# A planned attention and expert kernel: transfers booked in order, loads held back, v in rows of 128 tokens

## The chip, the core and the metric

The kernel runs on one NeuronCore of one Trainium2 chip. The core has a matrix engine (TensorE, PE in the profile, with its weight loads shown apart as PEld), a vector engine (VectorE, DVE), a scalar engine (ScalarE, ACT), a general engine (GpSimd, POOL) and SyncE (SP), which issues nearly all transfers here. The metric is device microseconds of one execution; lower is better. The kernel before took 566.9 us, the median of 3 runs from 564.42 to 567.85.

## The reference

Three layers follow each other; all inputs but the third layer's weights are float32.

1. Attention by landmarks, for 4 batches of 8 heads with 576 tokens and head size 64. 32 landmarks of q and of k are means over 18 tokens. With sm the softmax over scaled products: A = sm(q, k_lm), Bm = sm(q_lm, k_lm), C = sm(q_lm, k). Z is the inverse of Bm by six rounds of Z = 2Z - Z Bm Z. The result is A Z C v.
2. A layer of 8 experts. A router picks one expert for each of the 2304 tokens (rows of 512); each expert takes at most `capacity` tokens, in order. Its result is `relu(x w1) w2`, 512 to 1024 to 512, times the router's probability.
3. A gated unit on all rows: `(sigmoid(x w_gate) * (x w_val)) w_out`, 512 to 1536 to 512.

## The kernel before, in words

Each (batch, expert) pair that holds tokens is a unit of work: all 576 tokens of the batch are taken through that expert and the gated unit, and the rows that belong to the expert are scattered into `out`. In these inputs three such units show in the trace: "lead" (batch 0), "1" (batch 1) and "2". The lists of units are computed on the chip, and a loop at the end runs over what is left.

**Attention.** q and k of a batch come in four tiles of two transfers each (`load_qk`, `slot` tiles for batches 0 and 1, `qk` tiles for 2 and 3), v in one tile `vs` with one buffer (`load_v`). `sums` adds up the landmarks `ld`, `inverse` makes Bm (`pb`) and runs the six rounds (`pz`, tile `rz`), `context_parts` makes the scores of C (`pc`), `context_part` their exponentials (`ec`), `context_turn` transposes these with TensorE (`pct`) and copies them to SBUF (`ct`), and `context` multiplies them by v (`pv`). In the kernel before a tile row of `ct` and `vs` is one of 96 groups of 6 tokens, so that there are 2 x 3 transposes of 96 columns for each of two groups of heads, and 6 products for each head. `scores` and `weights` make A (`pa`, `ea`, `at`): maximum, subtraction, exponential, sum, normalisation and transposes. `back` joins Z and C v to `fold`, multiplies by the router's weights (`pw`) and gets each token's logits; `parts` splits A into two rounded parts that are the rows x of the expert layer (in the tiles `xa` and `xb` for batches 0 and 1), and `row_store` writes them and `fold` to memory, where a later unit reads them again.

**Lead experts.** `number` (`pl`) finds the expert of the first token of batch 0 and of batch 1. SyncE reads that number and loads the expert's 16 weight tiles of 256 KB (`expert_loads`, tile `w_raw`, four buffers). The first eight are multiplied by `fold` (`expert_fold`: products `mm<-w_raw,fold_now`), the others split into two rounded parts (`expert_split`, tile `ws`). `expert_products` then runs the hidden layer (`mm<-xa,ws`) and the w2 layer (`mm<-slot,ws`); `gated` scales its result by the gate (`yt`) and writes it over x in `xa`. So TensorE can work on the lead experts while the attention of the later batches is still under way. The third layer's weights are loaded, narrowed to float32 and used only after the attention (`narrow`, `unit_split`, `unit_products`, `unit_out`).

**The planner.** The order on each engine is written out by hand-made code, the class `Streams`. Each piece of work is a generator that yields the engine that it wants next and what it needs: names of events, or of buffers. `go` starts at every step the piece with the smallest sum of its possible start and `SLACK` (0.003 us) times its urgency, so 100 points of urgency are worth 0.3 us; a smaller number goes first. `settle` advances the engines' clocks by the costs in `COSTS`. A transfer is booked by `took("sp", ...)` and an event some fixed time later. An operation of GpSimd also costs VectorE 0.3 of its time (`SHARED`). `slow` guesses from the columns of recent products whether TensorE's clock would fall; then pieces marked `pe+` (dense products) go first, and `fill_up` puts products without use (`idle`) in front of a piece that would start late. The planner sets only the order: on the chip every instruction still waits for the data that it needs, and SyncE's queue runs in the order given.

Other names that matter: `SUBS` says which engine subtracts the maximum in `weights`, for each batch; `SUMS` which landmark sums run on GpSimd; `URGENCY` holds the urgencies.

Of the kernel before, what the change touches and what calls it, by code (L numbers as in the profile page):

```python
# [38 lines left out]
    lead_split=20,  # L39
    fold=0,  # L40
# [8 lines left out]
SUBS = ("pool", "pool", "dve", "dve")  # L49
NORMS = ("pool", "pool", "pool", "pool")  # L50
SLACK = 0.003
# [53 lines left out]
class Streams:  # L105
# [14 lines left out]
    MARGIN = 1.08  # L120
    SOON = 0.0
    SPAN = 3.4
    SHORTEST = 96

    def __init__(self, nc, slots):
# [6 lines left out]
        self.live = []  # L132
        self.busy = {}
# [19 lines left out]
    def took(self, engine, time):  # L153
        self.log.append(("run", engine, time, 0))

# [134 lines left out]
def tile_attention_moe_glu(  # L290
# [15 lines left out]
    B, P, H, J, DH = v.shape  # L306
    S = P * J
    N, D = out.shape
# [14 lines left out]
    REST = T % 128  # L323
    ENDS = [0, 1, *range(4, TC), 2, 3]
# [49 lines left out]
    nc.vector.tensor_reduce(eye, ident.rearrange("p (h m) -> p m h", m=LM), AX.X, ALU.add)  # L374
    shift = once.tile([128, 256], F32R, name="shift")
# [48 lines left out]
    def use(run):  # L424
        on.pe, on.dve, on.act, on.pool = run.pe, run.dve, run.act, run.pool
        on.later, on.took, on.release, on.done = run.later, run.took, run.release, run.done
# [59 lines left out]
    def gated(b, y, d, half, pt):  # L486
# [3 lines left out]
        yield "dve", "sg", f"gate_{b}"  # L490
# [32 lines left out]
    def narrow_all():  # L523
        for f in range(KG):
            cols = [w[f].bitcast(U32).rearrange("p k (f w) -> p k f w", w=2) for w in (w_gate, w_val)]
            rows = w_out[f].bitcast(U32).rearrange("p (k d w) -> p k d w", w=2, k=KD)
            for nm, res, src in zip("gvo", (wgs, wvs, wos), (*cols, rows)):
# [5 lines left out]
                on.took("sp", 2.1)  # L533
                on.done(f"raw_{nm}{f}", 2.5)
                run.spawn(narrow(res[f], raw, kind, f"{nm}{f}"), URGENCY["narrow"])

    def urgency(stage, b):
        if b == B - 1 and stage in ("inverse", "context", "back", "ranks"):
            return 0
        return URGENCY[stage] + (STEP * b - AHEAD * (b == 0) if b in range(B) else 0)  # L540
# [9 lines left out]
    def expert_loads(b, number, at, split_urgency, first=0, until=KF + 2 * KD, after=(), needs=()):  # L550
# [7 lines left out]
        for i in range(first, until):  # L558
# [8 lines left out]
            run.took("sp", 0.6)  # L567
            run.done(f"w_raw_{b}{i}", 2.2)
# [216 lines left out]
    def zero_rows():  # L785

        rows = out.rearrange("(p r) d -> p (r d)", p=128)
        for c in range(18):
# [6 lines left out]
            on.took("sp", 1.5)  # L795
# [7 lines left out]
    def block_x(b, number, x, *needs):  # L803
# [6 lines left out]
        on.took("sp", 2.5)  # L810
        for event in (f"fold_{b}", f"x_{b}0", f"x_{b}1", f"gate_{b}"):
            on.done(event, 6.0)
# [3 lines left out]
    with actx:  # L816
# [36 lines left out]
        def load_qk(b):  # L853
            for w, src in enumerate((q, k)):
                for g in range(G):
                    if b < 2:
                        t = slot(4 * b + 2 * w + g, F32)
                    else:
                        yield "sp", "qk"
                        t = wk.tile([128, 2, S], F32, tag="qk", name=f"qk{b}{w}{g}", bufs=6)  # L860
                    for kk in range(2):
                        yield ("sp",)
                        nc.sync.dma_start(t[:, kk], src[b, g, :, kk])
                        run.took("sp", 0.6)
                        run.done(f"raw{b}{w}{g}{kk}", 2.0)
# [9 lines left out]
        def load_v(b):  # L875
            yield "sp", f"raw{b}{1}{G - 1}1", f"context{b - 1}"
            vs = wk.tile([P, H, J, DH], F32, tag="vs", name=f"vs{b}", bufs=1)
            for h in range(0, H, 2):
                nc.sync.dma_start(vs[:, h : h + 2], v[b, :, h : h + 2])
            run.took("sp", 4.5)  # L880
            if b == 0:
                nc.sync.dma_start(wrt, w_router)
                nc.sync.dma_start(cap_i, capacity.bitcast(I32).partition_broadcast(128))
            st[b]["vs"] = vs
            run.done(f"v{b}", 2.0)
# [27 lines left out]
        def inverse(b):  # L913
# [52 lines left out]
            run.release("bank")  # L966
            yield ("dve",)
            dve.tensor_tensor(rz[:, :, 1], bb[:, 0], rn.unsqueeze(2).broadcast_to([128, G, LM]), ALU.mult)

            for it in range(NS_ITERS):  # L970
                last = it == NS_ITERS - 1
                yield "pe", "bank", *([f"square{b}{it - 1}"] if it else [])
                pr = pst([128, G, 2, LM], f"pz{b}{it}")
                for h in range(H):
                    o, g = (h % 4) * 32, h // 4
                    of = slice(1, 2) if last else slice(0, 2)
                    pe.matmul(pr[o : o + 32, g, of], rz[o : o + 32, g, 0], rz[o : o + 32, g, of], start=True, stop=True)
                new = wk.tile([128, G, LM] if last else [128, G, 2, LM], F32, tag="zl" if last else "rz", name=f"rz{b}{it}")
                if not last:
                    run.later([("act", lambda new=new, pr=pr: act.copy(new[:, :, 0], pr[:, :, 0]))], free(done=[f"square{b}{it}"]))  # L980
                yield ("dve",)
                dve.tensor_tensor(
                    new if last else new[:, :, 1], rz[:, :, 1], pr[:, :, 1], ALU.add if it else ALU.subtract
                )
# [66 lines left out]
        def context(b):  # L1051
            yield None, f"context{b - 1}"
            ct = st[b]["ct"] = wk.tile([P, G, 2, 3, 128], F32, tag="ct", name=f"ct{b}", bufs=1)
# [5 lines left out]
            for g in range(G):  # L1059
                for u in range(2):  # L1060
                    yield "pe", f"ct{b}{g}{u}", *(["bank"] if g == u == 0 else [])
                    if g == u == 0:
                        pv = pst([128, G, DH], f"pv{b}")
                    for jj in range(3):
                        for i in range(H // G):
                            o = place(H // G * g + i)[2]
# [43 lines left out]
        def context_part(b, g, pcs):  # L1110
# [8 lines left out]
            for u in range(2):  # L1119
                yield "act", "ec"  # L1120
                ec = wk.tile([128, HT], F32, tag="ec", name=f"ec{b}{g}{u}")
                act.activation(ec, pcs[u], AF.Exp, bias=nb, scale=SA, accum_out=sums[:, u : u + 1])
# [4 lines left out]
        def context_turn(b, g, u, ec):  # L1127
# [434 lines left out]
```

## Time and profile before

| | |
|---|---|
| median of 3 runs | 566.9 us (564.42 to 567.85) |
| profiled execution | 566.14 us |
| its span | 564.3 us, 12363 instructions |
| TensorE busy | 543.3 us, 96% (weight loads 489.7 us, 87%) |
| VectorE, ScalarE, GpSimd busy | 346.6 us (61%), 251.1 us (44%), 82.3 us (15%) |
| transfers | 61.86 MB, mean 110 GB/s |
| products without use (`idle`) | 18, 10.9 us, all before 27 us |

The profile is of one execution. Busy times are sums over instructions; matmuls are pipelined, so the span of a group of them divided by their count is the better price of one, and "mean ns" is how long one is in the pipe. The page's own chain of what ended last is short here, as it stops at the last scatter; the argument goes by stages instead.

### The profile page before, as it was taken

To read this page: it belongs to the slowest core of one execution; us is meant where nothing else is said; L and a number is where in the kernel's file an instruction comes from. 1 tells how busy PE (TensorE), PEld (TensorE's weight loads), DVE (VectorE), ACT (ScalarE), POOL (GpSimd) and SP (SyncE) were. 2 spreads that over 40 slices of the span, in tenths; PEclk is the share of its full clock that TensorE was granted. 3 is DMA by queue.
4 is the path that set the end of the run, shared out by engine and by line. 5 is a ranking of instruction groups with operands and counts; after the bars stand their busy time and mean duration, and the time that the engine had idled before them with its cause. 6 is when DMAs were issued, how large, how long until landed. Compare 5 with 4: busy or idle time off the path is not lost. (4 is left out here: it accounts for less than half of the span.)

```text
span 564.3 us, 12363 instructions
## 1 busy us (share of the span) xinstructions
PE 543.3 (96%) x4938; PEld 489.7 (87%) x4938; DVE 346.6 (61%) x824; ACT 251.1 (44%) x564; POOL 82.3 (15%) x100
## 2 busy tenths in 40 slices
PE   8889899999999999999999999999999999999994
PEld 3457768888998999999899999998999999999993
DVE  7877698877699988897453434343565534344431
ACT  1446434453577767674243333343443333333430
POOL 2662743242210000000120000001200000000012
PEclk9979899997999999999999999999999999999998
DMA  8998276685654544440520000002520000000002
GB/s 283 312 290 274 77 234 190 211 230 196 243 150 150 201 173 156 180 154 2 187 77 1 1 1 0 1 1 66 186 59 1 0 1 1 1 1 1 2 19 70
DMA packets 32479, 61.86 MB, mean 110 GB/s; under 512 B 3648, under 2 KB 13504, under 8 KB 32416
## 3 DMA queue, kind: packets, MB, share of 16 engines
q1 hardware_dynamic: 31312, 57.48, 32.2%
q0 software_dynamic: 1104, 3.54, 1.8%
q8 instruction: 40, 0.66, 0.5%
q14 instruction: 23, 0.19, 0.1%
HBM read 47.76 MB, written 13.25 MB: 108 GB/s over the span
## 5 line engine op out<-in xcount | busy, mean ns | idle before, releaser
L100 PE MATMUL mm<-xa,ws 128*128 128x288 f32 x1344 | 188.4, 297 | 0.9 <-ACT sg L100 0.8
L100 PEld LDWEIGHTS mm<-xa,ws 128*128 128x128 f32 x1344 | 183.3, 189 | 5.4 <-ACT sg L100 1.1
L100 PE MATMUL acc<-ws,slot 128*128 128x512 f32 x504 | 123.5, 392 | 0.0
L100 PEld LDWEIGHTS acc<-ws,slot 128*128 128x128 f32 x504 | 91.8, 188 | 17.5 <-issue 0.4
L100 PE MATMUL mm<-xb,ws 128*128 128x288 f32 x672 | 95.1, 300 | 0.0
L100 PEld LDWEIGHTS mm<-xb,ws 128*128 128x128 f32 x672 | 92.8, 192 | 1.7 <-PE mm L100 0.5
L100 PE MATMUL mm<-slot,ws 128*128 128x288 f32 x576 | 81.5, 298 | 0.0
L100 PEld LDWEIGHTS mm<-slot,ws 128*128 128x128 f32 x576 | 77.1, 188 | 2.8 <-issue 1.9
L100 ACT CAST slot<-sg 128x288 fp32r<-128x288 f32 x72 | 31.1, 432 | 66.7 <-DVE sg L100 66.4
L100 DVE TENSOR_TENSOR slot<-sg,slot 128x288 fp32r<-128x288 f32 (+2 forms) x108 | 35.4, 355 | 24.3 <-ACT slot L100 24.2
L100 DVE TENSOR_TENSOR sg<-mm,sg 128x288 f32<-128x288 f32 x72 | 32.7, 455 | 27.8 <-PE mm L100 20.4
L100 DVE TENSOR_TENSOR ws<-wo_res,ws 128x512 fp32r<-128x512 f32 x36 | 24.9, 692 | 35.4 <-ACT ws L100 35.4
L100 DVE TENSOR_TENSOR ws<-wg_res,ws 128x512 fp32r<-128x512 f32 x36 | 24.9, 691 | 27.1 <-ACT ws L100 27.1
L100 DVE TENSOR_TENSOR ws<-wv_res,ws 128x512 fp32r<-128x512 f32 x36 | 24.9, 691 | 24.5 <-ACT ws L100 24.3
L100 ACT CAST ws<-wo_res 128x512 fp32r<-128x512 f32 x36 | 22.4, 621 | 34.9 <-PE acc L100 28.4
L100 ACT CAST ws<-wg_res 128x512 fp32r<-128x512 f32 x36 | 22.3, 620 | 29.2 <-PE mm L100 28.4
L100 ACT CAST ws<-wv_res 128x512 fp32r<-128x512 f32 x36 | 22.3, 618 | 28.3 <-PE mm L100 27.4
L100 ACT ACTIVATE sg<-mm 128x288 f32<-128x288 f32 x72 | 29.0, 403 | 1.0 <-PE mm L100 0.9
L100 ACT ACTIVATE slot<-mm 128x288 fp32r<-128x288 f32 x48 | 19.6, 410 | 17.1 <-PE mm L100 16.5
L100 DVE TENSOR_TENSOR yt<-mm,gate_now 128x288 f32<-128x288 f32 x24 | 16.8, 701 | 16.7 <-PE mm L100 16.7
L770 POOL DMA_INDIRECT out<-o_tile,idx_two x5 | 4.8, 966 | 150.8 <-DVE o_tile L100 147.8
L100 POOL TENSOR_TENSOR ws<-w_raw,ws 128x512 fp32r<-128x512 f32 x16 | 20.9, 1304 | 37.3 <-ACT ws L100 37.3
(212 smaller groups left out, 541.4 us busy)
## 6 DMA issues: line engine op xcount, KB each, us to landing
w_raw<-in_moe_w SPq DMA_DIRECT2D x48, 256.0 KB, 4.6
raw_g<-in_moe_w_gate SPq DMA_DIRECT2D x12, 512.0 KB, 3.9
raw_v<-in_moe_w_val SPq DMA_DIRECT2D x12, 512.0 KB, 3.9
raw_o<-in_moe_w_out SPq DMA_DIRECT2D x12, 512.0 KB, 3.9
vs<-in_v SPq DMA_DIRECT2D x16, 288.0 KB, 7.6
out<-zeros SPq DMA_DIRECT2D x18, 256.0 KB, 3.7
slot<-in_q SPq DMA_DIRECT2D x8, 288.0 KB, 5.6
slot<-in_k SPq DMA_DIRECT2D x8, 288.0 KB, 5.7
```

What stands on the lines that cost most here:

```text
L100: return getattr(self.engine, op)(*args, **kwargs)
L770: scatter = nc.gpsimd.indirect_dma_start(out[:, :], bass.IndirectOffsetOnAxis(ap=idx[0:n, c : c + 1], axis=0), o[0:n], None, bounds_check= ...
```

## The change

1. The planner books transfers. `took("sp", ...)` and `done(event, delay)` of a transfer become `moved(bytes, *events)`: the transfer starts after the one before it, moves 0.36 MB per us and lands 0.64 us later; SyncE is booked until the eighth transfer before has landed (`LANES`).
2. Some transfers are held back (`HOLD`): q and k of batch 2 until the lead's weight tile 3 is in, those of batch 3 until tile 7, the row store of batch 0 until tile 15; that of batch 1 is not held.
3. Urgencies are other numbers, with an extra per batch (`EXTRA`), and `MARGIN`, by which `slow` asks for dense work, goes from 1.08 to 1.2.
4. `gated` waits for the row store of its batch before it writes over x ("rows0", "rows1").
5. The subtraction of the maximum goes to VectorE for batches 0 and 1 and to GpSimd for 2 and 3 (before: the other way round).
6. v is laid out on the host in order of tokens and loaded as rows of 512 numbers, 128 tokens to a tile row block, with three transfers a batch (512, 512 and 128 KB) for four of 288 KB. The context weights are turned in five transposes (four of 128 columns and one of 64) for six of 96, in two parts (`PARTS`), and multiplied by v in five products a head for six. `ec` is one tile for both halves.
7. A form of `inverse` in which TensorE also adds (`SQUARES`) is there but switched off ("dve" for all batches); a small tile `minus` belongs to it.

```diff
 URGENCY = dict(
-    load=150,
-    sums=60,
+    load=0,
+    sums=150,
     inverse=0,
-    scores=10,
-    context=10,
-    back=10,
-    weights=30,
-    ranks=20,
+    scores=5,
+    context=5,
+    back=-20,
+    weights=40,
+    ranks=-20,
     number=-20,
-    lead_rows=80,
-    rows=5,
-    lead_loads=5,
+    lead_rows=200,
+    rows=-50,
+    lead_loads=-300,
...
-SUBS = ("pool", "pool", "dve", "dve")
+SUBS = ("dve", "dve", "pool", "pool")
 NORMS = ("pool", "pool", "pool", "pool")
+SQUARES = ("dve", "dve", "dve", "dve")
+HOLD = (15, -1, 3, 7)
+EXTRA = dict(lead_loads0=-15, lead_loads1=-200, lead_rows0=-30, lead_split0=15, lead_split2=-200, lead_split3=-300, load0=200, load2=100, load3=-100, rows1=-100, sums0=30, sums1=-30, sums3=15, weights3=-15)
...
-    MARGIN = 1.08
+    MARGIN = 1.2
...
+    LANES = 8
+    RATE = 0.36
...
+            elif what == "move":
+                if not first and engine != "sp":
+                    at += self.LAG
+                first, engine = False, "sp"
+                at = max(at, self.free["sp"]) + 0.47
+                self.moving = max(at + 1.0, self.moving) + value * 1e-6 / self.RATE
+                self.landed = [*self.landed[1:], self.moving + 0.64]
+                for event in name:
+                    self.events[event] = self.landed[-1] + self.SHARED
+                self.free["sp"] = max(at, self.landed[0])
...
+    PARTS = ((0, 1), tuple(range(2, TC)))
...
-        yield "dve", "sg", f"gate_{b}"
+        yield "dve", "sg", f"gate_{b}", *{"lead": ["rows0"], "1": ["rows1"]}.get(b, [])
...
-                        yield "sp", "qk"
+                        held = [f"w_raw_lead{HOLD[b]}"] if HOLD[b] >= 0 else []
+                        yield "sp", "qk", *held
...
-            vs = wk.tile([P, H, J, DH], F32, tag="vs", name=f"vs{b}", bufs=1)
-            for h in range(0, H, 2):
-                nc.sync.dma_start(vs[:, h : h + 2], v[b, :, h : h + 2])
-            run.took("sp", 4.5)
+            vs = wk.tile([128, TC, D], F32, tag="vs", name=f"vs{b}", bufs=1)
+            for c in range(0, S // 128, 2):
+                rows = v[b, c * 128 : (c + 2) * 128]
+                nc.sync.dma_start(vs[:, c : c + 2], rows.rearrange("(c p) d -> p c d", p=128))
+                run.moved(4 * 256 * D)
+            nc.sync.dma_start(vs[0:REST, TC - 1], v[b, S - REST : S])
+            run.moved(4 * REST * D, f"v{b}")
...
-                    for jj in range(3):
+                    for c in PARTS[part]:
+                        n = TILES[c][1]
                         for i in range(H // G):
...
                             pe.matmul(
                                 pv[o : o + 32, g],
-                                ct[:, g, u, jj, o : o + 32],
-                                vs[:, 4 * g + i, 2 * jj + u],
-                                start=(u == jj == 0),
-                                stop=(u == 1 and jj == 2),
+                                ct[0:n, g, c, o : o + 32],
+                                vs[0:n, c, h * DH : (h + 1) * DH],
+                                start=(c == 0),
+                                stop=(c == TC - 1),
                             )
...
-            pt = pst([P, 3, 128], f"pct{b}{g}{u}")
-            for jj in range(3):
-                pe.transpose(pt[:, jj], ec[:, jj * P : (jj + 1) * P], ident)
-            run.release("ec")
+            pt = pst([128, len(PARTS[part]), 128], f"pct{b}{g}{part}")
+            for i, c in enumerate(PARTS[part]):
+                t0, n = TILES[c]
+                pe.transpose(pt[0:n, i], ec[:, t0 : t0 + n], ident)
+            if part:
+                run.release("ec")
...
-            run.copy(st[b]["ct"][:, g, u], pt)
+            run.copy(ct[:, g, first : first + 2], pt[:, 0:2])
+            if part:
+                yield ("any",)
+                run.copy(ct[0:REST, g, TC - 1], pt[0:REST, 2])
...
-            yield "sp", f"scaled{b}0", f"scaled{b}1", f"fold{b}0", f"fold{b}1"
+            held = [f"w_raw_{lead_rows[b][0]}{HOLD[b]}"] if b < LEADS and HOLD[b] >= 0 else []
+            yield "sp", f"scaled{b}0", f"scaled{b}1", f"fold{b}0", f"fold{b}1", *held
```

## Rows read from the trace of the kernel before

**Rows 1.** Busy us and instructions of each engine, granted clock and transfers, by stage.

```profile
core 0: us, PE busy (x) PEld busy (x) DVE busy (x) ACT busy (x) POOL busy (x), PEclk, DMA share, GB/s
0.00:43.04 43.04, 35.13 (x641) 19.01 (x641) 32.87 (x112) 15.00 (x49) 21.87 (x44) 0.92 0.96 294
43.04:142.01 98.97, 94.54 (x1463) 80.26 (x1459) 77.96 (x240) 46.81 (x131) 38.87 (x36) 0.95 0.66 200
...
167.45:545.00 377.55, 376.64 (x2598) 355.70 (x2597) 212.26 (x432) 170.26 (x348) 10.13 (x10) 1.00 0.18 60
```

**Rows 2.** Order of time, TensorE: start, length, work, count, and the idle time before it.

```profile
20.45 0.55 PE L100 MATMUL pz<-rz 32*32 32x64 f32 x16 [1.42 <-DVE rz L100]
...
37.79 0.64 PE L100 MATMUL mm<-w_raw,fold_now 64*32 64x128 f32 x16
...
43.04 2.65 PE L100 MATMUL mm<-xa,ws 128*128 128x288 f32 x18
45.62 1.20 PE L100 MATMUL pc<-qk,ld 64*32 64x288 f32 x32
...
142.01 25.60 PE L100 MATMUL mm<-slot,ws 128*128 128x288 f32 x192
```

**Rows 3.** Busy time and granted clock, three stretches and a lull.

```profile
28.00:38.00 10.00, 9.57 (x214) 6.30 (x218) 7.17 (x23) 5.92 (x22) 8.98 (x11) 0.66 0.91 316
58.00:66.00 8.00, 6.29 (x65) 5.53 (x65) 3.54 (x13) 2.88 (x9) 6.34 (x7) 0.79 0.17 48
126.00:136.00 10.00, 8.58 (x59) 7.66 (x58) 6.45 (x22) 2.64 (x7) 2.39 (x2) 0.66 0.67 237
...
26.00:28.00 2.00, 1.00 (x33) 0.48 (x32) 1.74 (x8) 0.49 (x2) 0.79 (x1) 1.00 1.03 264
```

**Rows 4.** TensorE's waits: who, for whom, us in total, times, longest.

```profile
PE pv L100 <- issue: 2.2, 2, 1.8
PE mm L100 <- DMA w_raw<-in_moe_w: 2.1, 3, 0.8
...
PE pk L100 <- DVE rsum L100: 1.4, 1, 1.4
PE pc L100 <- DMA qk<-in_k: 1.2, 2, 0.7
```

**Rows 5.** Order of time, SyncE's issues; last, issues from 140 to 260 us.

```profile
32.99 1.94 SPq L565 DMA_DIRECT2D w_raw<-in_moe_w  x4
35.02 2.69 SPq L879 DMA_DIRECT2D vs<-in_v  x4
...
44.65 1.73 SPq L1368 DMA_DIRECT2D x_rows<-xa  x2
...
56.48 15.98 SPq L565 DMA_DIRECT2D w_raw<-in_moe_w  x4
...
w_raw<-in_moe_w SPq DMA_DIRECT2D x2, 256.0 KB, 2.8
```

**Rows 6.** Two lines in order of time, TensorE; last, the copies by tile.

```profile
90.90 0.82 PE L100 MATMUL pct<-ident,ec 128*96 128x128 f32 x6
91.65 1.62 PE L100 MATMUL pv<-vs,ct 96*32 96x64 f32 x96
...
L100 ACT COPY ct<-pct x16: 463/481/499, 16.6 to 91.9; 96x384 f32<-96x384 f32 x16
```

**Rows 7.** Order of time, GpSimd and VectorE.

```profile
19.07 1.15 POOL L100 TENSOR_TENSOR ea<-ea,ma 128x576 f32<-128x576 f32 x1
19.32 0.99 DVE L100 TENSOR_TENSOR rz<-bb,rn 128x64 f32<-128x64 f32 x1
...
105.79 0.21 DVE L100 TENSOR_TENSOR rz<-bb,rn 128x64 f32<-128x64 f32 x1
...
106.23 0.75 DVE L100 TENSOR_TENSOR ea<-ea,ma 128x576 f32<-128x576 f32 x1
```

**Rows 8.** The store's issues with us to landing; first write over x rows, ScalarE.

```profile
x_rows<-xa SPq DMA_DIRECT2D x2, 576.0 KB, 6.0
...
77.47 0.43 ACT L100 CAST xa<-yt 128x288 fp32r<-128x288 f32 x1 [1.88 <-DVE yt L100]
```

More of the change, by code (lines that the diff above doesn't have):

```diff
@@ L132, in __init__ @@
         self.live = []
+        self.moving = 0.0
+        self.landed = [0.0] * self.LANES
         self.busy = {}
@@ L154, in took, with moved @@
         self.log.append(("run", engine, time, 0))
+    def moved(self, size, *events):
+        self.log.append(("move", events, size, 0))
     def release(self, *kinds):
@@ L305, in tile_attention_moe_glu @@
     nc = tc.nc
-    B, P, H, J, DH = v.shape
-    S = P * J
-    N, D = out.shape
+    B, S, D = v.shape
+    N = out.shape[0]
+    DH = q.shape[2] // 2
+    H = D // DH
+    J = 6
+    P = S // J
     E, F = w1.shape[0], w1.shape[1] * w1.shape[4]
@@ L374, in tile_attention_moe_glu @@
     nc.vector.tensor_reduce(eye, ident.rearrange("p (h m) -> p m h", m=LM), AX.X, ALU.add)
+    minus = once.tile([128, LM], F32, name="minus")
+    nc.vector.tensor_scalar_mul(minus, eye, -1.0)
     shift = once.tile([128, 256], F32R, name="shift")
@@ L425, in use @@
         on.pe, on.dve, on.act, on.pool = run.pe, run.dve, run.act, run.pool
-        on.later, on.took, on.release, on.done = run.later, run.took, run.release, run.done
+        on.later, on.took, on.release, on.done, on.moved = run.later, run.took, run.release, run.done, run.moved
     on = SimpleNamespace()
@@ L538, in urgency @@
         if b == B - 1 and stage in ("inverse", "context", "back", "ranks"):
-            return 0
-        return URGENCY[stage] + (STEP * b - AHEAD * (b == 0) if b in range(B) else 0)
+            return EXTRA.get(f"{stage}{b}", 0)
+        return EXTRA.get(f"{stage}{b}", 0) + URGENCY[stage] + (STEP * b - AHEAD * (b == 0) if b in range(B) else 0)
     def free(*kinds, done=()):
@@ L566, in expert_loads @@
             w_raw[b, i] = raw
-            run.took("sp", 0.6)
-            run.done(f"w_raw_{b}{i}", 2.2)
+            run.moved(4 * 128 * D, f"w_raw_{b}{i}")
     def expert_fold(b, at, first, until, *needs):
@@ L794, in zero_rows @@
             )
-            on.took("sp", 1.5)
+            on.moved(4 * 128 * n)
         on.done("zeroed")
@@ L809, in block_x @@
         nc.sync.dma_start(gate_now, gate_dram[bass.ds(at, 1)].rearrange("b p j -> b (p j)").broadcast_to([128, S]))
-        on.took("sp", 2.5)
-        for event in (f"fold_{b}", f"x_{b}0", f"x_{b}1", f"gate_{b}"):
-            on.done(event, 6.0)
+        on.moved(4 * 128 * (H // 2 * LM + 2 * G * T + S), f"fold_{b}", f"x_{b}0", f"x_{b}1", f"gate_{b}")
     stage = ctx.enter_context(tc.tile_pool(name="stage", bufs=3))
@@ L966, in inverse @@
             run.release("bank")
+            by = rn.unsqueeze(2).broadcast_to([128, G, LM])
             yield ("dve",)
-            dve.tensor_tensor(rz[:, :, 1], bb[:, 0], rn.unsqueeze(2).broadcast_to([128, G, LM]), ALU.mult)
+            if SQUARES[b] == "act":
+                dve.scalar_tensor_tensor(rz[:, :, 1], bb[:, 0], -1.0, by, ALU.mult, ALU.mult)
+            else:
+                dve.tensor_tensor(rz[:, :, 1], bb[:, 0], by, ALU.mult)
             for it in range(NS_ITERS):
                 last = it == NS_ITERS - 1
-                yield "pe", "bank", *([f"square{b}{it - 1}"] if it else [])
+                both = SQUARES[b] == "act"
+                yield "pe", "bank", *([f"square{b}{it - 1}"] if it and not both else [])
                 pr = pst([128, G, 2, LM], f"pz{b}{it}")
@@ L976, in inverse @@
                     of = slice(1, 2) if last else slice(0, 2)
-                    pe.matmul(pr[o : o + 32, g, of], rz[o : o + 32, g, 0], rz[o : o + 32, g, of], start=True, stop=True)
-                new = wk.tile([128, G, LM] if last else [128, G, 2, LM], F32, tag="zl" if last else "rz", name=f"rz{b}{it}")
[L979 to L984, printed above, removed]
+                    pe.matmul(
+                        pr[o : o + 32, g, of], rz[o : o + 32, g, 0], rz[o : o + 32, g, of],
+                        start=True, stop=not both,
+                    )
+                    if both:
+                        pe.matmul(
+                            pr[o : o + 32, g, 1], (eye if it else minus)[o : o + 32], rz[o : o + 32, g, 1],
+                            start=False, stop=True,
+                        )
+                new = wk.tile([128, G, LM] if last else [128, G, 2, LM], F32, tag="zl" if last else "rz", name=f"rz{b}{it}")
+                if both:
+                    yield ("act",)
+                    act.copy(new, pr[:, :, 1] if last else pr)
+                else:
+                    if not last:
+                        run.later([("act", lambda new=new, pr=pr: act.copy(new[:, :, 0], pr[:, :, 0]))], free(done=[f"square{b}{it}"]))
+                    yield ("dve",)
+                    dve.tensor_tensor(
+                        new if last else new[:, :, 1], rz[:, :, 1], pr[:, :, 1], ALU.add if it else ALU.subtract
+                    )
                 run.release("bank")
@@ L1336, in gate @@
             nc.sync.dma_start(gate_dram[b], gates[:, b])
-            run.took("sp", 0.6)
-            run.done(f"gate{b}", 3.0)
+            run.moved(4 * S, f"gate{b}")
             if b < LEADS:
@@ L1375, in row_store @@
             run.done(f"rows{b}")
-            run.done(f"x{b}", 6.0)
         def block_list():
```

45 lines of the change are left out of this document (25 added, 20 removed).

## The prediction

> **What bounds the kernel now.** I read first the busy time by stage [rows 1]. Its boundaries come from the order of TensorE's work [rows 2]: at 43.04 us the first product of the lead expert runs, and at 142.01 us the second lead's w2 products begin, 25.6 us without a break. From 167.45 to 545 TensorE is busy for 376.6 of 377.6 us at a granted clock of 1.00. The change leaves the work behind 142 us as it is, so this part and the tail after it only slide. All that can be won or lost lies ahead: TensorE is busy for 35.1 of 43.0 us in the first stage and for 94.5 of 99.0 us in the second, at clocks of 0.92 and 0.95. The DMA share is 0.96 in the first and 0.66 in the second, where VectorE is busy for 78.0 of the 99.0 us.
>
> [...]
>
> That view, what TensorE waited for [rows 4], is short: 2.1 us for the lead expert's weights, 1.2 for k of batch 3, 1.4 for VectorE's rsum, and 2.2 put down to "issue". Transfers by name are 3.3 us, not the whole prize.
>
> Last I read the order of TensorE and SyncE up to the lead expert [rows 2, 5]. SyncE issues its first weights at 32.99, their first fold runs at 37.79, the first product at 43.04. Four of batch 2's v transfers (35.02, 2.69 us of issuing) stand behind the fourth weight transfer, and the store of x rows, 2 x 576 KB, at 44.65 among those that follow.
>
> **The change, part by part.** The sum is made against the profiled execution: a span of 564.3 us and 1.8 us around it, 566.1 us in all, 0.8 us under the median of 566.9.
>
> **Fewer products.** The context weights take 5 transposes for 6, twice a batch: 40 for 48. The v products go from 384 instructions to 320. Six transposes ran in 0.82 us, 137 ns each, and 96 v products in 1.62 us, 17 ns each [rows 6]. 8 x 137 + 64 x 17 ns = 2.2 us. The half of it in batches 0 and 1 mostly precedes 43.04, where the weights set the pace, so the bounds are -1.1 and -2.2 us; I take **-1.5**, between them, as some of batch 1's products stand in the way of the lead's folds. The copies of these weights become 24 for 16, none wider than before: at 481 ns each [rows 6] at most 3.8 us more on ScalarE, which is busy for 46.8 of 99.0 us [rows 1] and covers them; they would count only where v products wait for a copy. The row of minus signs runs before the first data land: 0. SyncE issues 12 v transfers for 16, each 0.67 us by the row at 35.02, on a queue that waits for buffers anyway: 0.
>
> **Earlier lead.** q and k of batch 2 now wait for the lead's fourth weight transfer, those of batch 3 for the eighth, the store of x rows for the sixteenth, and the lead's loads come first. From issue to first fold took 4.8 us; on a quieter queue such a transfer lands in 2.8 [rows 5]: 2.0 us. The waits for weights between the folds (2.1 us) could go too. And in batch 0's inverse TensorE waited 1.42 us [rows 2] for rz, an operation of 0.99 us against 0.21 in batch 3 [rows 7]: it ran beside a subtraction on GpSimd and ended just after it. That subtraction moves to VectorE, up to 0.8 us on the lead's chain. The ends are 0 (other loads fill the queue as well) and -4.9; I take **-3.5**, nearer the far end, because these waits lie in the chain that ends last there. Behind the held loads on SyncE stands v of batch 2, and for them waits batch 2's context, whose first products ran at 45.62 [rows 2]. Its q and k, 8 x 288 KB at the 294 GB/s of the first stage [rows 1], take 8 us, so from some 36 us on they are down at 45, and those products come about 8 us later; the lead's own products stand in for them. If they did not, this would cost up to the 8 us.
>
> **Holes and clock after 43 us.** The waits of 1.8, 1.2 and 1.4 us and the two slow stretches (1.7 and 3.4) are 9.5 us. The new order can shut them: it books landings, and its wider margin brings dense products forward or fills idle time. But the 1.8 us ended with nothing that a plan of transfers knows, and the 1.4 with VectorE. Bounds: -9.5, and +3.5 for one more hole of 1.8 us with a slow stretch of 1.7. I take about half of the gain, **-4.5**.
>
> **The swapped subtractions.** VectorE gives up four (batches 2, 3) and takes four (0, 1), 0.75 us each [rows 7]: 0. But GpSimd now runs four of 1.15 us in the midst of the lead's work. A VectorE operation that meets one can lose 0.99 - 0.21 = 0.78 us. Bounds 0 and 4 x 0.78 = +3.1; VectorE has 21 us to spare in that stage, so I take **+0.5**.
>
> [...]
>
> **The guarded rows.** The lead's output overwrites x rows in xa, so its first write must follow the store that now comes after the sixteenth weight transfer. That transfer was issued by 72.46; with 1.73 us of issuing the store (the row at 44.65) and a landing of 6.0 it would be down at 80.2, while the first write stood at 77.47 [rows 8]. That is a wait of 2.7 us on ScalarE, and behind it in that queue come weight splits and batch 2's exponentials. ScalarE idled 1.88 us right there, and TensorE had w2 products. Bounds 0 and +2.7: **+0.5**.
>
> Sum: -1.5 - 3.5 - 4.5 + 0.5 + 0.5 = -8.5. From 566.1 that gives 557.6, from the median 558.4; I say **558**. All gains at their best (-2.2 - 4.9 - 9.5 = -16.6) give 549.5.
>
> **The rivals.**
>
> *The holes move.* A new order has late results of its own: VectorE stays loaded, and an "issue" gap can open anywhere. Then the fewer products (-1.1) and part of the earlier lead (-1.5) remain: 564. For it speaks that the two largest holes were not caused by transfers; against it, that the lead's waits for weights were.
>
> *The guarded write stalls the lead.* Slower than before: ScalarE, held at the first write to xa, keeps back the weight splits for the next w2 products, and TensorE stops until the store has landed. The price is 1.7 + 6.0 us and then a slow stretch of 3.4 us: +11.1, less 1.5 for the products, from 566.1: 575.7. It decides if TensorE runs out of split weights before the landing: two w2 products (24 matmuls each, at 25.6 us / 192 = 0.13 us) last 6.4 us, so if the store is issued together with the first of them or later. Against it: TensorE has seven PSUM banks, and attention work of batches 2 and 3 to put in between.
>
> *Nothing happens.* The transfers that matter were hidden, and what is won early is waited out later: 567. Against it stand the 2.1 us for weights, which nothing covered.
>
> **Chances.** The forecast (549 to 562) 0.55, holes that move (562 to 567) 0.28, nothing 0.07, the stalled write 0.10. The range for eight in ten reaches from 549 to 568. About 1% is what a measurement of this kernel can tell from no change, here 561.2 to 572.6. Faster 0.55: what of the forecast lies over 561.2 and what of the second case falls below it cancel. Same 0.35, slower 0.10.
>
> **What would show it.** Right: the first product on xa before 41 us; 40 transposes and 320 v products; no v transfer among the lead's first eight weights; the slow stretches after 43 us under half of their 5.1 us; the second lead's w2 products without a break from about 134 us. Wrong: a first product at 43 us or later; the holes back under other names; a long wait of ScalarE ahead of its first cast into xa with TensorE idle beside it; or a stage behind 142 us that is no longer full, because the narrowing of the third weights, VectorE's work there, began late.

## The result, and the profile after

The changed kernel takes 559.8 us (median of four runs, 559.0 to 560.6) against 565.7 us for the kernel before in the same session: a ratio of 0.989 with an interval of 0.985 to 0.994. A second measurement of it, in the experiments below, gave 0.993 (0.990 to 0.996). The forecast of 558 us and its range hold; the change is worth about one per cent. Which of its parts earned that came out otherwise than forecast.

The profiled execution took 559.3 us with a span of 557.5. Busy time by stage, as in [rows 1], from its own boundaries: the first lead product (40.57, before 43.04) and the start of the dense work behind the second lead (161.42, before 167.45).

```profile
0.00:40.57 40.57, 34.51 (x598) 18.69 (x598) 33.71 (x116) 15.23 (x54) 13.99 (x32) 1.00 0.63 214
40.57:161.42 120.85, 118.21 (x1636) 103.47 (x1633) 91.29 (x267) 59.94 (x161) 54.18 (x53) 0.99 0.71 234
161.42:538.30 376.88, 376.80 (x2601) 356.19 (x2600) 214.09 (x437) 172.23 (x352) 10.13 (x10) 1.00 0.19 63
```

The first stage is 2.5 us shorter, the stretch to the dense work 3.6 (124.4 to 120.9), and the rest 0.8: together the 6.8 us between the spans 564.3 and 557.5. The granted clock is 1.00 and 0.99 where it was 0.92 and, from 43.04 to 167.45, 0.96, and the transfers' share of the first stage fell from 0.96 to 0.63. In the first stage the planner also put in more products without use: 30 of 15.0 us in all, the last at 38.0 us, for 18 of 10.9 us, the last at 25.8. They fill gaps of TensorE in the stretch where it ran slow before.

TensorE in order of time, to be set against [rows 2]:

```profile
22.36 0.43 PE L103 MATMUL pz<-rz 32*32 32x64 f32 x16
...
36.52 1.19 PE L103 MATMUL mm<-w_raw,fold_now 64*32 64x128 f32 x32 [0.31 <-DMA w_raw<-in_moe_w]
...
40.57 1.86 PE L103 MATMUL mm<-xa,ws 128*128 128x288 f32 x12
...
141.50 20.08 PE L103 MATMUL mm<-slot,ws 128*128 128x288 f32 x150
161.42 5.72 PE L103 MATMUL mm<-xa,ws 128*128 128x288 f32 x42
```

The first inverse product comes 1.9 us later than before, the first fold 1.3 earlier.

TensorE's waits, against [rows 4]:

```profile
PE pa L103 <- DVE yt L103: 2.5, 1, 2.5
PE idle L103 <- POOL ident masks.py:199: 1.9, 1, 1.9
PE mm L103 <- DMA w_raw<-in_moe_w: 1.2, 3, 0.7
```

The holes named before ("issue", rsum, k of batch 3) are gone. One of 2.5 us is new. In order of time, VectorE and TensorE, it looks like this:

```profile
74.91 0.96 DVE L103 TENSOR_TENSOR xa<-yt,xa 128x288 fp32r<-128x288 f32 x1 [4.78 <-DMA x_rows<-xa]
75.80 0.64 DVE L103 TENSOR_TENSOR yt<-mm,gate_now 128x288 f32<-128x288 f32 x1
...
76.49 0.71 PE L103 MATMUL pa<-qk,ld 64*32 64x288 f32 x14 [2.50 <-DVE yt L103]
77.14 0.68 PE L103 MATMUL pv<-vs,ct 128*32 128x64 f32 x24
77.74 4.18 PE L103 MATMUL mm<-slot,ws 128*128 128x288 f32 x18
```

VectorE's first write over the x rows stands 4.78 us for the row store. Behind it on VectorE waits the product with the gate, which empties a PSUM bank, and TensorE waits for that. The 18 products behind the hole take 232 ns each, the 150 at 141.50 take 134: the hole is followed by a slow stretch, the only one in this trace ahead of 552 us (granted clock 0.50 from 77.94 to 81.35). It stands at the lead's first writes over x, where [rows 8] have that of before.

### The profile page after: what moved, and what is told of

Read it like the earlier page. It is cut to its first block, busy times and chain, and to the rows that moved or that the text cites. A ratio compares the mean times of both kernels' runs of the same rounds, so it can differ in the third digit from the quotient of the medians.

```text
span 557.5 us, 12250 instructions
## 1 busy us (share of the span) xinstructions
PE 540.5 (97%) x4878; PEld 487.2 (87%) x4878; DVE 342.7 (61%) x826; ACT 249.9 (45%) x571; POOL 83.1 (15%) x100
## 5 line engine op out<-in xcount | busy, mean ns | idle before, releaser
L103 PE MATMUL mm<-xb,ws 128*128 128x288 f32 x672 | 93.9, 296 | 0.0
L103 PEld LDWEIGHTS mm<-xb,ws 128*128 128x128 f32 x672 | 90.9, 188 | 2.1 <-issue 0.5
L103 PEld LDWEIGHTS mm<-slot,ws 128*128 128x128 f32 x576 | 78.5, 191 | 1.7 <-issue 0.5
L103 ACT ACTIVATE slot<-mm 128x288 fp32r<-128x288 f32 x48 | 19.5, 409 | 15.4 <-PE mm L103 15.2
L103 DVE SCALAR_TENSOR_TENSOR slot<-mm,slot 128x288 fp32r<-128x288 f32 x48 | 21.4, 450 | 6.9 <-ACT slot L103 6.4
```

What stands on the lines that cost most here:

```text
L103: return getattr(self.engine, op)(*args, **kwargs)
```

## The experiments

Where nothing else is said, a kernel keeps the changed kernel's order on every engine and alters one thing. Where only that order is edited, the code cut tells the edit in words. All ran on one chip but four (all but v, v's transfers by themselves, the old transfers' time, the new plan); a ratio is always to the kernel before on the same chip in the same session. A trace shows one execution, and its time is given where it lies far from the median. Each execution also has its mean granted clock: (1 - clock) x span is called here what it lost to the clock.

**The changed kernel again.** No edit; it is what the next three are set against.

> The changed kernel unaltered, as the yardstick for the others of this group: about 559.8 us, ratio to the kernel before 0.989, by every theory. The wait of some 2.5 us ahead of a pa product near 74 us, with a slow stretch behind it, should be there again.

560.7 us (559.7 to 562.4), ratio 0.993 (0.990 to 0.996). In its trace the new hole is 3.6 us, and there is a gap of 1.5 us put down to "issue" ahead of an inverse product at 48.6 that the first trace of the same kernel does not have. Such gaps come and go between executions of one program; the last section says what they follow.

**The lead's rows in tiles of their own**, so that no write has to wait for the store (the small tile `spots`, used after the attention, shares the buffer of `ct` to make room):

```diff
+x0 = [wk.tile([128, G, 2, HT], F32R, name=f"x0{tag}") for tag in ("xs", "x0")]
-run.spawn(expert_products(name, x, x, ROLL_LEAD, ...
+run.spawn(expert_products(name, x if b else x0, x, ROLL_LEAD, ...
```

> The order of all instructions is that of the changed kernel; the lead expert's x rows (batch 0) lie in two tiles of their own, not in xa, so that its first output need not wait for the store of those rows. Theory 'guarded write': VectorE's 4.8 us of waiting for that store near 70 to 75 us go, and with them TensorE's 2.5 us of idling and the slow stretch behind (1.7 us): 4.2 us less than the changed kernel, about 555.6. Rival 'VectorE is late anyway': the wait comes back under another name (another result of VectorE or ScalarE) in the same place, and the time falls by less than 1.5 us, to 558.3 or more.

554.6 us (554.4 to 558.9, five of six under 555.1), ratio 0.983 (0.980 to 0.987): 6.1 us less than the changed kernel beside it, and the fastest version here. The stretch around the hole, first in the changed kernel run beside it, then in this one:

```profile
72.00:86.00 14.00, 10.45 (x166) 8.13 (x165) 8.72 (x22) 3.22 (x9) 6.69 (x8) 0.88 0.75 260
```

```profile
72.00:86.00 14.00, 14.00 (x243) 11.35 (x243) 13.33 (x41) 5.74 (x18) 8.94 (x10) 1.00 0.78 259
```

Busy time and clock are both back: 3.55 us of hole and (1 - 0.88) x 14 = 1.7 us of slow stretch, 5.2 of the 6.1 us. By ratio the gain is 0.94%, or 5.3 us.

**An earlier store** for the same wait: the store of batch 0 behind the lead's eighth weight, not its sixteenth.

```diff
-SyncE: ... w_raw 8 ... w_raw 16, x_rows of batch 0
+SyncE: ... w_raw 8, x_rows of batch 0 ... w_raw 16
```

> The order of the changed kernel, but SyncE issues batch 0's store of x rows right behind the lead's eighth weight transfer and not behind its sixteenth. Theory 'guarded write': VectorE's wait for the store and TensorE's 2.5 us with the slow stretch go (4.2 us), and the 1.2 MB in front of the ninth weight costs little, since TensorE has the folded products by then: 555.6 to 557. Rival 'the store belongs behind the weights': weights nine to sixteen land some 4 us later, TensorE waits for them, and the gain is eaten: 559 or more.

558.8 us, ratio 0.989 (0.986 to 0.992), 1.9 us less than the changed kernel. That lies between the two forecasts. The hole is gone here too, and another, of 1.8 us, stands earlier in the trace (up to 52.02 us), with a slow stretch of 1.7 us behind it:

```profile
PE pz L158 <- ACT rz L158: 1.8, 1, 1.8
```

**Nothing held back**: q and k of batch 2 and q of batch 3 right behind v of batch 1, with the lead's rows in xa and (second) in tiles of their own.

```diff
 SyncE: v of batch 1
+SyncE: q, k of batch 2, q of batch 3
 SyncE: w_raw 1 to 4 of the lead, ...
```

> The order of all engines but SyncE is that of the changed kernel; on SyncE q and k of batch 2 and q of batch 3 are issued right behind v of batch 1, as in the kernel before, and not after the lead's weights. Theory 'held loads clear the queue': the lead's weights land in 4 to 5 us again for 3.0, the first fold comes at 38 or later for 36.5, TensorE waits 2 us or more for weights, the first lead product comes at 42.5 to 43 for 40.6, and the whole takes 2 us more than the changed kernel, about 561.8. Rival 'the lead's weights are covered': the first product comes within 0.5 us of 40.6 and the time stays within 0.8 us of 559.8.

> The changed kernel's order with the lead's rows in tiles of their own (554.6 us before this run) and q and k of batch 2 and q of batch 3 issued right behind v of batch 1 again. It prices the held transfers without the guarded write in the way. Theory (the lead's landing sets the first stage): with them ahead of the lead's weights the first product of the lead runs about 3 us later, at 43 us for 40, TensorE idles for it, and the time is 2 to 3.5 us longer, 556.6 to 558. Rival (the attention of batch 2 fills the gap and all is caught up before the second lead): the first product is late too, but the time stays within 0.8 us of 554.6.

In xa: 561.0 us, ratio 0.993 (0.989 to 0.996), no different from the changed kernel, though in its trace (563.9 us, the slowest of the seven runs) the first lead product came at 43.50. In tiles of their own: 557.5 us (555.2 to 559.7), ratio 0.986 (0.981 to 0.990), 2.8 us above its partner; the two intervals overlap. In that trace (559.7 us, the slowest of the six) TensorE stands 2.6 us in an "issue" gap, runs slow behind it, and the first fold comes at 42.51 where the held kernel has 35.98. The third row is the busy time around it:

```profile
PE pgt L158 <- issue: 2.6, 1, 2.6
```

```profile
42.51 1.71 PE L158 MATMUL mm<-w_raw,fold_now 64*32 64x128 f32 x32
```

```profile
36.00:44.00 8.00, 7.48 (x95) 4.21 (x90) 5.16 (x19) 1.29 (x6) 0.00 (x0) 0.57 0.33 120
```

In these traces the holds bring the lead forward by some 3 us or more. In the time, with the guarded write out of the way, they are worth what shows here, 2.8 us by medians and 0.24% by ratio, which the intervals do not tell from nothing.

**The subtractions swapped back**, with the lead's rows in tiles of their own:

```diff
-SUBS = ("dve", "dve", "pool", "pool")
+SUBS = ("pool", "pool", "dve", "dve")
```

> Order and tiles as above, transfers held as in the changed kernel, but the row-maximum subtractions of batches 0 and 1 go to GpSimd again and those of batches 2 and 3 to VectorE, as before the change. It prices the swap. Theory of the prediction (the swap costs 0.5 us, and takes 0.8 us off batch 0's inverse): within 1 us of 554.6. Rival (an operation of VectorE that meets one on GpSimd waits until it is over, so four subtractions in the midst of the lead's work cost up to 4.6 us): without them there it is 2 us or more faster, under 552.6. Third: 2 us or more slower, because the 0.99 us of rz in batch 0 lies on the chain of the first stage.

556.0 us, ratio 0.983 (0.979 to 0.987), equal to the kernel without this edit by ratio (0.983) and 1.3 us above it by medians, between the forecasts. The swap cannot be told from nothing, and the rival (2 us faster) fell. In batch 0 rz takes 0.15 to 0.16 us either way, here with the subtraction on GpSimd: in the new order the two no longer meet.

```profile
21.79 0.16 DVE L158 TENSOR_TENSOR rz<-bb,rn 128x64 f32<-128x64 f32 x1
```

**v alone**: the kernel before in its own order, with v in rows of 128 tokens, five transposes, 320 products and three copies a pair (part 6 of the change and nothing else).

> The kernel before in its own order, held back nowhere, with v in rows of 128 tokens and the context weights turned in five products: the fewer products alone, to be set against the kernel before. Prediction: 1.5 us faster (1.1 to 2.2), a ratio of 0.997. Rival (a v product over 128 rows takes some 22 ns where one over 96 took 17, so that 320 of them cost what 384 did): -0.3 to 0 us, a ratio of 0.9995 to 1. Third: slower by over 1 us, because there are three copies of context weights where there were two, and v products wait for the last.

558.8 us (556.7 to 562.1), ratio 0.9885 (0.984 to 0.993). This one part gives all that the whole change gives, more than four times the forecast for it. Its TensorE rows and waits:

```profile
39.29 4.03 PE L156 MATMUL mm<-xa,ws 128*128 128x288 f32 x18
...
134.71 25.60 PE L156 MATMUL mm<-slot,ws 128*128 128x288 f32 x192
```

```profile
PE pk L156 <- DVE rsum L156: 1.4, 1, 1.4
PE mm L156 <- DMA w_raw<-in_moe_w: 0.9, 1, 0.9
```

The same 192 products begin at 134.71, not 142.01. Of these 7.3 us TensorE's idle time up to there gave 3.5 (12.3 to 8.8) and its busy time 3.8 (129.7 to 125.9). In the waits, "issue" (2.2) is gone and the weights' wait fell from 2.1 to 0.9; the hole of 1.4 is still there. The clock over windows of 2 us loses 5.1 us where it lost 8.5. The other executions say the same: their mean is 6.7 us below that of the kernel before, and of this 3.7 us is what they lost to the clock (5.4 for 9.1), so that 3.0 us is something else.

**All but v**: the changed kernel's order and holds, with the old form of v.

```diff
-vs = wk.tile([128, TC, D], F32, tag="vs", ...)
+vs = wk.tile([P, H, J, DH], F32, tag="vs", ...)
```

> The changed kernel's order and holds, with v in 96 rows, six transposes and 96 v products again: all of the change but v. Theory (v's form is worth some 7 us, the rest about nothing with its guarded write): 565 to 568, not faster than the kernel before. Rival (the order brings its own 5 to 6 us, and v's form little in it, since the held transfers leave the queue half idle while v lands): 560 to 562.

566.7 us (563.0 to 570.3), against 566.6 for the kernel before: 1.002 (0.999 to 1.005). Planner, holds, swap and guarded rows together are worth nothing that shows. The lead comes a little earlier, and the hole at the guarded write stands against it (the trace is of 563.7 us, the second quickest of the twelve):

```profile
42.12 1.85 PE L158 MATMUL mm<-xa,ws 128*128 128x288 f32 x12
```

```profile
PE pa L158 <- DVE yt L158: 3.7, 1, 3.7
```

The two ratios multiply to 0.990, the measured change. This kernel and the changed one have one order, so their product rows, TensorE before 180 us, compare like with like; this one first:

```profile
L158 PE MATMUL pv<-vs,ct 96*32 96x64 f32 x384 | 8.6, 228 | 1.0 <-DMA vs<-in_v 0.8
L158 PE MATMUL pct<-ident,ec 128*96 128x128 f32 x48 | 7.0, 278 | 0.0
```

```profile
L103 PE MATMUL pv<-vs,ct 128*32 128x64 f32 (+1 forms) x320 | 7.9, 225 | 0.0
L103 PE MATMUL pct<-ident,ec 128*128 128x128 f32 (+1 forms) x40 | 6.4, 283 | 0.0
```

15.6 us of products became 14.3: 1.3 us.

**v's transfers by themselves.**

```diff
+for form in (96 x 3 KB, 128 x 2 KB, 96 x 2 KB, 128 x 3 KB, 128 x 2.25 KB, 96 x 3 KB, 128 x 2 KB):
+    load v of four batches in this form; reduce_max over all of it
```

> Nothing of the computation: only v is loaded, all four batches (4.72 MB), seven times over, each time followed by a maximum on VectorE that waits for all of it. Forms in order: 96 rows x 3 KB (as before), 128 rows x 2 KB (as changed), 96 x 2 KB, 128 x 3 KB, 128 x 2.25 KB, then the first and the second again. The queue's share of time fell from 32.2% of 564.3 us to 31.0% of 557.3 us when v alone took its new form, 8.9 us for these bytes. Theory (a transfer over 96 rows is moved at three quarters of the rate of one over 128): the three forms over 96 rows take 4 us or more longer than the others, whatever the bytes of a piece. Rival (the size of the pieces counts): 96 x 2 KB goes as 128 x 2 KB. Third (neither: alone on the queue all forms run at one rate within 5%, and the difference is in how they share it with q, k and weights).

Loaded bytes per second tell the forms apart. Windows inside the third to the seventh form (VectorE, GpSimd, clock, DMA share, GB/s):

```profile
64.00:80.00 16.00, 0.00 (x0) 0.00 (x0) 1.00 1.00 271
95.00:109.00 14.00, 0.00 (x0) 0.00 (x0) 1.00 0.92 337
121.00:134.00 13.00, 0.00 (x0) 0.00 (x0) 1.00 0.99 355
146.00:163.00 17.00, 0.00 (x0) 0.00 (x0) 1.00 0.99 274
179.00:192.00 13.00, 0.34 (x1) 0.00 (x0) 1.00 1.03 347
```

And the loads' ends, as the maximum's start:

```profile
81.07 12.95 DVE L318 TENSOR_REDUCE peak<-vc 96x1 f32<-96x12288 f32 x1 [19.35 <-DMA vc<-in_v]
...
109.70 9.75 DVE L318 TENSOR_REDUCE peak<-vd 128x1 f32<-128x9216 f32 x1 [15.68 <-DMA vd<-in_v]
...
134.86 9.75 DVE L318 TENSOR_REDUCE peak<-ve 128x1 f32<-128x9216 f32 x1 [15.41 <-DMA ve<-in_v]
...
144.65 11.98 SPq L317 DMA_DIRECT2D vf<-in_v  x16
164.14 12.95 DVE L318 TENSOR_REDUCE peak<-vf 96x1 f32<-96x12288 f32 x1 [19.52 <-DMA vf<-in_v]
...
177.12 0.91 SPq L326 DMA_DIRECT2D vg<-in_v  x2
193.50 10.82 DVE L330 TENSOR_REDUCE peak<-vg 128x1 f32<-128x10240 f32 x1 [14.17 <-DMA vg<-in_v]
```

From first issue to the maximum, v over 96 rows takes 19.5 us (3 KB pieces) or 19.3 (2 KB), over 128 rows 15.4 to 15.7, in the changed kernel's form 193.50 - 177.12 = 16.4. The size of the piece does nothing, the number of rows a fifth; in the form used, with its 64 rows at the end, it is a sixth, 3.1 us for four batches. The forecast of 4 us or more was right in kind and a little high: its three quarters would make 96 rows take 4/3 of the time of 128, and the trace gives 19.4 / 15.5 = 1.25. Why the rows count, the trace does not show.

**The time of the old transfers, with the new products**: v alone as above, and 256 KB more behind v's second transfer of each batch.

```diff
+nc.sync.dma_start(spare, v[b, 0:128])
 nc.sync.dma_start(vs[0:REST, TC - 1], v[b, S - REST : S])
```

> The kernel before with v in rows of 128 tokens, as in the run that gave 558.8 us, and behind the second v transfer of each batch 256 KB more, read into a tile that nobody uses: at 347 GB/s (128-row form, alone on the queue) 0.75 us a batch, 3.0 us in all, about what the 96-row form took longer (19.5 against 16.4 us for four batches). Products and copies stay those of the new form. Theory (the shorter transfers made the gain): most of it is gone, 562 to 566 us, and the lead's first product comes at 40.5 us or later, not 39.3. Rival (the gain lay in the products and copies): within 1.5 us of 558.8, up to 560.3, with a first product near 39.3.

558.1 us (556.4 to 561.0), ratio 0.987 (0.983 to 0.992), as without the extra bytes. The lead is 0.8 us later and the second lead 1.0, in a trace of 559.9 us:

```profile
40.12 2.65 PE L156 MATMUL mm<-xa,ws 128*128 128x288 f32 x18
...
135.66 25.60 PE L156 MATMUL mm<-slot,ws 128*128 128x288 f32 x192
```

So half of the queue's time, put back, takes nothing of the gain away; my theory (562 to 566) fell. The test is not complete, since the extra bytes restored 4.7 us of the queue's busy time (31.8% of 558.1 us against 31.0% of 557.3) and the old form has 8.9 more.

**A hole filled in the kernel before**: two products of the second lead ahead of the ranking products that wait 1.4 us for rsum.

```diff
-TensorE: pk (ranks), ..., mm<-xb x48
+TensorE: mm<-xb x48, pk (ranks), ...
```

> The kernel before, with two products of the second lead's expert (48 matmuls, 6 us) moved ahead of the first ranking products, which waited 1.4 us for rsum and were followed by a stretch at a granted clock of 0.66 (3.4 us lost). Theory (that hole cost its wait and the slow stretch behind it): 4 to 5 us faster than the kernel before, 559.7 to 560.7 against 564.6. Rival (only the wait is won, and the slow stretch comes elsewhere): 1.4 us or less. Third: not faster, because the ranking products, 6 us later, hold up what follows them.

567.3 us (563.3 to 572.9), ratio 1.004 (1.001 to 1.008): not faster. The profiled execution, the quickest of the twelve, shows the second lead's run 3.4 us earlier than in [rows 2]; it has another gap of the "issue" kind ahead of v's last two products, as the kernel before has at 59.71:

```profile
60.08 0.27 PE L156 MATMUL pv<-vs,ct 96*32 96x64 f32 x2 [0.94 <-issue]
...
138.63 25.60 PE L156 MATMUL mm<-slot,ws 128*128 128x288 f32 x192
```

What the longer executions did instead, no trace shows, but their clocks do: the twelve lost 11.0 us to the clock in the median, the kernel before 9.6, and the longer executions had the lower clocks (572.9 us at 0.975, 563.3 at 0.986). A wait of 1.4 us with 3.4 us of slow clock behind it could not be cashed by moving work in front of it.

**A new plan for the lead's own tiles**: the planner run again without the wait for the store.

```diff
-yield "dve", "sg", f"gate_{b}", *{"lead": ["rows0"], "1": ["rows1"]}.get(b, [])
+yield "dve", "sg", f"gate_{b}", *{"1": ["rows1"]}.get(b, [])
```

> The lead's rows in tiles of their own and the planner run anew, without the wait for the store ahead of the lead's first write. Theory (that wait was all that the rows cost; a plan without it is as good): 553 to 556. Rival (an order found with the wait in it was a lucky one, and a new plan has holes of its own): 557 or more.

559.3 us (556.3 to 560.4), ratio 0.987 (0.983 to 0.991), by ratio 0.3% above the order kept from the changed kernel; the intervals overlap. Its trace keeps the clock at 1.00 to 161 us and still begins the dense work 4.4 us later (161.16 against 156.72): idle time of 2.1 us for 0.1 behind the first lead product, and 2.5 us more of busy time. That the kept order was partly a lucky one is likely from this, but not shown.

## Why the prediction was right, and where not

**What failed: v's transfers at nothing.** The prediction took "SyncE issues 12 v transfers for 16 ... on a queue that waits for buffers anyway: 0" and saw in v's new form only products, at -1.5. As TensorE time the products are right: -1.3, inside -1.1 to -2.2. But the form as a whole is worth 6.5 us by its ratio (0.0115 x 565.9), more than the whole change. The transfers are a sixth quicker, the wait for the lead's weights is 1.2 us shorter, the "issue" gaps at v's products (2.2 us, 1.4 in the trace with the hole filled) are absent from both traces with the new form in the old order, and 3.4 us less go to slow stretches. Shown is that part 6 does it. Not shown is by which link: extra bytes did not undo it, and the gaps' places (last section) point to TensorE's instructions as much as to v. Untried is 96-row transfers with 128-row products.

**Earlier lead, -3.5 taken.** The first product came 2.5 us earlier, before 41, as called for. But v alone brings it to 39.29 and the order without v only to 42.12 from 43.04. Of the three sources, the wait for weights between folds fell (2.1 to 1.2), the first landing fell (4.8 to 36.52 - 33.56 = 3.0), and the inverse went wrong: its first product is at 22.36, later than 20.45, though rz itself is free. The 2.0 us of landing were credited to the holds; most of it v gives as well (3.4 us from issue to first fold there). And one thing is in no term of the sum: the slow stretch from 28 to 38 us that cost (1 - 0.66) x 10 = 3.4 us [rows 3]. In the changed kernel it is gone (the clock is 1.00 up to 40.57); so it is without v's new form (1.00 up to 42 us), where the lead came only 0.9 us earlier.

**Holes and clock, -4.5 taken.** The 1.7 and 3.4 us of slow stretches are (1 - clock) x length, (1 - 0.79) x 8 from 58 us and (1 - 0.66) x 10 from 126 us [rows 3]; the waits of 1.8 and 1.4 us [rows 4] stand ahead of them. Between the two traces this term is larger than half: idle time behind the first product fell by 1.8 us and the slow stretches after 43 us from 5.1 to 1.7, under half as the prediction asked. The trace of all but v has 1.7 us of slow stretches as well, but it is one of that kernel's quickest executions: over all twelve it lost 7.6 us to the clock in the median, the kernel before beside it 9.0, the changed kernel 4.5 and 5.6 in its two measurements, v alone 4.7. So most of the gain at the clock came with v's form and not with the order. A new hole came as the bound of +3.5 had it, only longer: 2.5 to 3.7 us with 1.7 behind it. Of the signs named, one failed: the second lead's w2 products were to begin at about 134 us, and they began at 141.50 (142.01 before); what came 6.0 us earlier is the dense work behind them. And the 1.8 us that, as the prediction put it, "ended with nothing that a plan of transfers knows" are tied to transfers after all, by their times: they end 1.35 us after a transfer of instructions (last section).

**Guarded rows, +0.5 taken: mis-sized.** It is 6.1 us by medians, 5.3 by ratio. The mechanism of that rival was right in place and kind: the first write waits, and TensorE stands behind it. Two details were not. VectorE waits, not ScalarE (ScalarE had written its row at 73.27), 4.78 us and not 2.7; and TensorE's stop is 2.5 to 3.7 us with a slow stretch, not 7.7. "TensorE had w2 products" did not cover it, since the next in the order written out was attention's `pa`: it ran at 76.49 after the 2.50 us, and 18 w2 products stood behind it, run from 77.74.

**Swapped subtractions, +0.5 taken**: nothing that can be told. Four subtractions on GpSimd at their full 1.15 us [rows 7], 4.6 us as the rival of that experiment had it, do not show in the time: the ratio is 0.983 with them in the midst of the lead's work and without. Single rows do show an operation of VectorE that ends about 0.1 us after one of GpSimd beside it. In the kernel before `rz<-bb,rn` took 0.99 us at 19.32 [rows 7], and 1.15 at 83.18 beside a weight split's subtraction of 1.32 from 82.92; in the changed kernel `bb` took 1.06 us at 78.47 beside one of 1.28 from 78.16, and 0.18 to 0.22 in the other batches. What in the chip makes it so, the traces do not show.

**The sum** of -8.5 against -5.9 measured: the guarded write alone is more than the shortfall. That the forecast came within 2 us of the time is luck: two errors met, v taken too small and the order too large.

## What to carry to other kernels

Price a change of layout by its transfers as well as its products: look at how many rows a transfer covers (alone on the queue, 271 to 274 GB/s over 96 rows and 337 to 355 over 128), and measure the part alone before crediting a scheduler. When a buffer is used again for output, look at what stands behind the guarded write in the written order: here the write waited 4.78 us and TensorE 2.50 behind it; a tile of its own, for 5 to 6 us of 560, was the best buy here. Closing one hole in a trace promises little unless the same work is shown to come earlier in the median: with the hole of 1.4 us filled, the kernel before took 567.3 us, a ratio of 1.004.

## What was not expected of the hardware

- A transfer over 96 rows moved 271 to 274 GB/s alone on the queue, one over 128 rows 337 to 355, at the same busy share of the DMA engines (0.92 to 1.03): here the busy share did not tell the throughput.
- Gaps of TensorE put down to "issue", 0.4 to 2.6 us, come and go between executions of one program, but not their places. Counted by the rows in order of time, the products that TensorE had issued ahead of each gap were:

| kernel | products ahead of a gap (its time, us) |
|---|---|
| before | 472 (0.41), 980 (1.80) |
| a hole filled | 219 (1.23), 852 (0.41), 980 (0.94) |
| changed, again; subtractions back | 721 (1.45); 721 (1.18) |
| nothing held back, in xa; in own tiles | 469 (1.17); 469 (2.55) |

  The work at these places differs, and the counts lie near steps of 127 products: 219 and then 2, 4, 5 and 6 steps on. So a gap seems to belong to a place in TensorE's list of instructions. The page of the kernel before counts a weight load for each of its 4938 products, so that 127 products are 254 instructions, and lists 40 transfers of the kind "instruction" on one queue, 16 KB each. If these serve TensorE, as the times below suggest, each brings 2 x 4938 / 40 = 247 instructions, an estimate from the page's counts, near the 254.

  The traces' records of single transfers tie the gaps to these. Each of the nine gaps ends 1.35 to 1.58 us after one of the 40 has ended; the waits of TensorE that have another releaser end anywhere from 0.0 to 13 us after. And whether such a transfer is late goes with the holds: in the seven traces with held transfers the DMA engines stand idle (share 0.00, without the instruction transfers) in the microsecond after the 346th product, and the third instruction transfer starts 0.2 to 1.1 us after that product; in the six without holds the share is 1.05 or 1.06, and it starts 2.3 to 4.0 us after. Two of the six (nothing held back) differ from the changed kernel, or its form with own tiles, in SyncE's order alone. The gaps at 469 and 472 products, which follow that transfer, are all among the six. By these times I take a gap of this kind for a wait for instructions whose transfer came late among those of data; no row of a trace names it so. That v's old form made the one at 980 products late is not shown: the transfer before that place started 22 and 78 products ahead of it in the two traces with a gap there, and 92 and 42 ahead in the two with v's new form in the old order, which have none.

  Four of the seven gaps over 0.9 us were followed by a stretch at a granted clock near 0.5 (0.50 from 62 to 64 us in the kernel before), three by none.
- One kernel's runs agreed within 0.7 us in five of six (tiles of their own, no slow stretch in the trace), those of the kernel before spread over 5 to 9 us in each session, and there the longer executions had the lower clocks (568.35 us at 0.977, 560.57 at 0.994).
